# Five moves of work in a fused FFT and SoLU kernel: the last chunk's halves in one step, a fold ahead of a product, and an opening in another order

## The chip, the cores and the metric

The kernel runs on one core of a Trainium2 chip. All numbers are device microseconds (us) of that core. A core has five engines that run their own instruction queues: TensorE (PE in the profile, its weight loads PEld), VectorE (DVE), ScalarE (ACT), GpSimd (POOL) and SyncE (SP), which here only issues DMAs. An engine works through its queue in order and waits on semaphores of the others. PSUM is the memory that TensorE writes to, in banks; SBUF is the working memory.

## The reference

```python
def _attn_ref(x):                       # x: (8, 3136, 256) float32
    X = np.fft.fft(x, axis=1)
    X = np.fft.fft(X, axis=2)
    return X.real.astype(np.float32)
...
def _moe_ref(x, w_in, w_out, g_ln):     # x: (25088, 256), w_in: (256, 1024), w_out: (1024, 256)
    h = x @ w_in
    h_max = np.max(h, axis=-1, keepdims=True)
    e = np.exp(h - h_max)
    sm = e / (np.sum(e, axis=-1, keepdims=True) + 1e-09)
    solu = h * sm
    mu = np.mean(solu, axis=-1, keepdims=True)
    var = np.mean((solu - mu) ** 2, axis=-1, keepdims=True)
    ln = (solu - mu) / np.sqrt(var + 1e-06) * g_ln
    return (ln @ w_out).astype(np.float32)
```

The real part of a two-dimensional Fourier transform of eight sequences is followed by a feed-forward layer with softmax gating and a layer norm.

## The kernel before

The 3136 positions of a sequence are 49 by 64, so the long transform is done in two stages. The eight sequences are taken as four pairs (`Pair`, p = 0 to 3).

**First stage.** A pair's input comes in eight chunks of four rows (c = 0 to 7). For each chunk `load` (L117) brings the rows `xa` (a DMA of SP) and their mirror image `xb` (an indirect DMA of POOL). `add_mirror` adds the two, `fold` or `fold_part` (L164) folds the features on DVE into `y`, and `transform1` (L184) multiplies half a chunk by the table F on PE (L216) and copies the PSUM bank to `z` on ACT (L219). A pair has 16 half chunks. After a chunk's second half `keep` (L223) writes z to a DRAM tile `zd`, a DMA of SP. `turn` (L226) reads it back in another arrangement as five frequencies per tile `g`, four DMAs, usually issued by POOL (L232).

**Second stage and layer.** A pair has 25 frequencies k1, and each of these is a `Unit`, 100 in all; a unit has two signs of the frequency (one sign where k1 = 0), 128 rows each. `transform2` (L234) makes q from g on PE (L244), `take2` (L248) copies it by ACT, `spread` (L252) turns one row of q into a column r by a 0.5 KB DMA on SP. `up` (L267) multiplies q by the input weights, even part c = 0 and odd part c = 1, into two PSUM tiles h0 and h1 (L272). On DVE `even` (L275, row L278) makes ev from h0, `join` (row L286) adds and subtracts h1 and finds the extremes, ACT takes the exponential (`expo`, L294), DVE multiplies (`product`, L301), ACT squares (`square`, L308), and `stats` and `power` make the scales. DVE turns blocks of 32 by 32 (`turn_both`, L372) into a tile v, and `move_blocks` (L396) sets 16 DMAs on SP (L408) that bring the blocks of two units to their places in uT. Two tiles of tag v and two of tag uT exist.

**The way down.** From the sixth step on a unit with two signs is multiplied by the output weights in seven block products instead of eight (`Down`, p1 to p7, L446); `sums` (L433, row L439) makes their operands on POOL, `keep_p`, `keep_x`, `keep_c` and `finish` scale the results into ot, and `store` writes them out: 1 SP DMA or, for two units together, 4, and for the other sign an indirect DMA of POOL (L531).

**Order.** `tc.manual_schedule()` keeps the written order on every engine. An opening prepares the weights (`Weights`: `exponent_*`, `confine` on ACT, `narrow_*` on DVE, products of the weights in `product_in`) while pair 0 goes through the first stage. Its z goes through places that are free then: chunks 2 and 3 stand in the tile `z_u` of tag u, which `expo` uses later, 4 and 5 in the weight sums `Ws`, 6 in a tile of S, 7 in a tile of g. Then one loop step per unit: steps 0 to 4 (`WHOLE` = 4) in a simple form, where `begin(i + 1)` starts the next unit, and from step 5 a pipelined form, in which step i does the up product of unit i, transforms unit i + 2, and does the way down of unit i - 5 between them; moves of blocks stand in even steps. The last step of the simple form, step 4, ends with a `fold_part` of pair 1's first chunk, behind the transposes.

**Other pairs.** The next pair's first stage is laid into the steps by a table:

```python
    SUMS = [None] + [[f + 2 * c for c in range(NC)] for f in (3, 27, 53)]
    ...
    def ahead_pe(pr, i):
        for c in range(NC):
            half = i - SUMS[pr.p][c] - 3
            if half in (0, 1):
                transform1(pr, c * CH // 2 + half)
    ...
        at = (-4, -3, 1, 6, 11)      # turn_parts: steps of `turn`, counted from the pair's first unit
```

For pair 1 the halves of the last chunk stand in steps 20 and 21, the first `turn` in step 21, and `transform2` of its first unit, 25, in step 23. For pair 3 these are steps 70, 71, 71 and 73, and for pair 2 they are 44, 45, 46 and 48.

Of the kernel before, what the change touches and what calls it, by code (L numbers as in the profile page):

```python
# [9 lines left out]
FP32 = mybir.dt.float32  # L10
# [7 lines left out]
P = 128  # L18
# [6 lines left out]
ZR = 4 * NK  # L25
CH = 4
NC = NH // CH
# [16 lines left out]
def kernel(  # L44
# [19 lines left out]
    nc = tc.nc  # L64
# [40 lines left out]
    def result(i):  # L105

        return banks[i % 4]
# [76 lines left out]
    def transform1(pr, s):  # L184

        c, l = divmod(2 * s, CH)
        if s == 0:
            pr.zd = dram.tile([ZR, NH, D], FP32, tag="zd", name="zd")  # L190
        if l == 0:

            if pr.p or c < 2:
                pr.z = zpool.tile([ZR, CH, D], FP32, tag="z", name="z")
            elif c < 4:
                if c == 2:
                    pr.z_u = fpool.tile([P, 2, FF], FP32, tag="u", name="z_u", bufs=1)
                pr.z = pr.z_u[0:ZR, c - 2].rearrange("p (l d) -> p l d", l=CH)
            elif c < 6:
                pr.z = Ws.rearrange("p (h w) c k -> h p (w c k)", h=2)[c - 4, 0:ZR].rearrange("p (l d) -> p l d", l=CH)  # L200
            elif c == 6:
                pr.z = S_tiles[1][0:ZR, 0:2].rearrange("p a c k -> p (a c k)").rearrange("p (l d) -> p l d", l=CH)
            else:
                pr.z = gpool.tile([P, KG, D], FP32, tag="g", name="z_g")[0:ZR, 0:CH, :]
            pr.zs[c] = pr.z
        y = pr.y[c]
        ps = result(0 if pr.p else s).rearrange("p (l d) -> p l d", l=2)
        if s == NH // 2 - 1:
            parts = [(ps[0:ZR, 0], y[:, l], 0), (ps[0:ZR, 1], pr.y0[:, 0], 1), (ps[0:ZR, 1], y[:, l + 1], 2)]
        else:  # L210
            parts = [(ps[0:ZR], y[:, l : l + 2], 0)]
        pr.done.append(s)
        first = True
        for o, i, t in parts:
            for h, cs in enumerate((EVEN, ODD)):
                nc.tensor.matmul(o[..., cs], F[:, 2 * t + h, :], i[..., cs], start=first, stop=True,  # L216
                                 skip_group_check=True)
                first = False
        nc.scalar.copy(pr.z[:, l : l + 2, :], ps[0:ZR])  # L219
        if l == CH - 2:  # L220
            keep(pr, c, slice(0, ZR if pr.p else 4 * KG))
# [30 lines left out]
    def spread(t):  # L252

        t.r = small.tile([P, 1], FP32, tag="r", name="r")
        nc.sync.dma_start(out=t.r, in_=t.q[0:1, P : 2 * P])
# [3 lines left out]
    class Unit:  # L259


        def __init__(self, p, k1):
            self.p, self.k1 = p, k1
            self.signs = (0, 1) if k1 else (0,)
            self.h, self.u, self.ot = [None] * 2, [None] * 2, [None] * 2

    def up(t, c):  # L267

# [6 lines left out]
    def even(t, ps):  # L275

        t.ev = fpool.tile([P, FF], FP32, tag="ev", name="ev", bufs=1)
        nc.vector.scalar_tensor_tensor(out=t.ev, in0=w_mid, scalar=t.r, in1=ps,  # L278
                                       op0=ALU.mult, op1=ALU.add)
# [298 lines left out]
    def confine(unit, here=False):  # L578

        if unit is None:  # L580
            return
        if here:
            bits(unit, unit, -896.0, ALU.add, 0.0, ALU.max)
            bits(unit, unit, 255.0, ALU.min, 2.0 ** 23, ALU.mult)
            return

        u = unit.bitcast(FP32)
        nc.scalar.activation(out=u, in_=unit, func=ACT.Relu, bias=limits[:, 0:1])
        nc.scalar.activation(out=u, in_=u, func=ACT.Relu, bias=limits[:, 1:2], scale=-1.0)  # L589
        nc.scalar.activation(out=unit, in_=u, func=ACT.Identity, bias=limits[:, 2:3], scale=-(2.0 ** 23))  # L590
# [22 lines left out]
    class Weights:  # L613
# [40 lines left out]
        def product_in(self, h):  # L654
            ps = ps_h.tile([P, FF], FP32, tag=f"h{h % 2}", name="wps")
            for half in range(2):
                fs = slice(half * HW, (half + 1) * HW)
                for c in range(KD):
                    lhsT = self.m[:, c, :] if h == KD else self.Q[:, c, h * P : (h + 1) * P]
                    nc.tensor.matmul(ps[:, fs], lhsT, self.w_in[c][:, fs], start=(c == 0), stop=(c == KD - 1))  # L660
            nc.scalar.copy(w_mid if h == KD else Wi[:, h, :], ps)

        def place_out(self):
# [50 lines left out]
                          mybir.DependencyInfo(mybir.DependencyClass.Sync, mybir.DependencyReason.DATA),  # L714
                          reason="two operands at a time from SBUF")

    def ahead_pe(pr, i):

        for c in range(NC):
            half = i - SUMS[pr.p][c] - 3  # L720
            if half in (0, 1):
                transform1(pr, c * CH // 2 + half)

# [6 lines left out]
    with tc.manual_schedule():  # L730
# [30 lines left out]
        for c in range(NC):  # L761

            if c == 0:
                weights.narrow_in(0)
                weights.narrow_in(1)
            elif c < 3:
                weights.narrow_in(c + 1)
            if c < 2:
                weights.exponent_in(c + 2)
            add_mirror(first, c, nc.vector)  # L770
            fold(first, c)
            if c == NC - 1:
                for i in range(3):
                    weights.exponent_out(i)
            if c + 6 < NC:
                load(first, c + 6)
            if c == 3:
                weights.place_out()
                for i in range(2):
                    weights.load_out(i)  # L780
                weights.load_table(0)
                weights.mid()
                weights.scale_out()
            for s in range(CH // 2):
                transform1(first, c * CH // 2 + s)
            if c == 3:
                weights.product_in(0)

        turn(first, 0, nc.sync, 0, 2)
        turn(first, 0, nc.gpsimd, 2, KG)  # L790

        confine(weights.units[0], True)
        for i in range(1, 3):
            confine(weights.units[i])
        weights.product_in(1)
        weights.narrow_out(0)
        weights.exponent_out(3)
        weights.product_in(2)
        for i in range(1, 3):
            weights.narrow_out(i)  # L800

        units = [Unit(p, k1) for p in range(NP) for k1 in range(NK)]
        for t in units[:2]:
            take2(t, transform2(pairs[0], t.k1))
            spread(t)
        confine(weights.units[-1])
        for c in (2, 3, 0, 1, 4, 5, 6, 7):
            keep(first, c, slice(4 * KG, ZR))
        weights.load_table(1)
# [3 lines left out]
        def second_transform(i):  # L813
            if i < len(units):
                t = units[i]
                take2(t, transform2(pairs[t.p], t.k1))
                spread(t)

        def enter(i):
            cur = units[i]  # L820
# [4 lines left out]
        def begin(i):  # L825

            cur = units[i]
            enter(i)
            even(cur, up(cur, 0))
            cur.odd = up(cur, 1)  # L830
            second_transform(i + 2)

# [7 lines left out]
        for i in range(whole + 1):  # L840
            cur = units[i]
            prv = units[i - 1] if i else None
            if prv:
                turn_whole(prv)
            for s in cur.signs:
                join(cur, s)
            if prv and i < whole:
                for o, ps in prv.wait:
                    nc.vector.tensor_copy(out=o, in_=ps)
            for s in cur.signs:  # L850
                expo(cur, s)
            if prv and i == whole:
                for o, ps in prv.wait:
                    nc.scalar.copy(o, ps)
            if i == 0:

                weights.narrow_out(3)
            for s in cur.signs:
                product(cur, s)
                if i < whole and s == 0:  # L860
                    square(cur, s)
            if i == 1:
                weights.centre()
                weight_sums()
            if i < whole:

                begin(i + 1)
                if 1 in cur.signs:
                    square(cur, 1)
                stats(cur)  # L870
                power(cur)
            else:
                for s in cur.signs:
                    square(cur, s)
                other_pairs(i, ahead, "mirror", cur)
                turn_both(cur)
                stats(cur)
                power(cur)
            if i == 0:
                turn(first, 1, nc.sync)  # L880
            for work in ("mirror", "fold", "load") if i < whole else ("fold", "load"):
                other_pairs(i, ahead, work)

        def by_seven(i):
# [6 lines left out]
        for i in range(whole + 1, len(units) + lag + 1):  # L891
# [31 lines left out]
            if seven:  # L923
                new.p6()
                new.keep_x()
                new.p2()
                new.keep_c()
            elif old:
                for s, ps in plain:
                    scale(old, s, ps)  # L930
            if prv and prv.batch.shared and prv.w:
                prv.batch.mix()
            if cur:
# [119 lines left out]
```

## Time and profile before

| | us |
|---|---|
| three runs | 1149.07, 1149.42, 1147.12 (median 1149.07) |
| the profiled execution | 1150.92 |
| its span, first to last instruction | 1149.1 |
| PE busy | 1098.1 |
| DVE busy | 993.0 |
| ACT busy | 799.3 |
| POOL busy | 799.9 |

Busy time is what an engine's instructions took; the span is what all engines share, so 51 us of it are without a matmul. The mean granted TensorE clock of the execution is 0.994 of full speed. A step is measured from one unit's first up matmul (L272) to the next one's. Between disturbances it lasts 10.13 us, 11.00 us with a half chunk of the first stage in it, and 11.45 us with the last half chunk, which has six matmul operations in place of two.

### The profile page before, as it was taken

The numbers are of one execution on the slowest core, as the hardware profiler recorded it, in microseconds if no ns is written. First come the engines' busy times: TensorE is split into PE (matmuls) and PEld (weight loads), VectorE is DVE, ScalarE is ACT, GpSimd is POOL, SyncE is SP. The second block draws the span as 40 slices with busy tenths as digits, with TensorE's granted clock in tenths as the row PEclk, the third lists the DMA queues.
The fourth block names the chain that finished last, engine by engine and source line by source line (L and its number), as shares of the span: only waits on it lengthen the run. The fifth ranks groups of instructions, "written<-read, shape, count | busy, mean of one in ns | idle before, by whom it ended". The sixth has DMA issues, their size and how long they took to land.

```text
span 1149.1 us, 21936 instructions
## 1 busy us (share of the span) xinstructions
PE 1098.1 (96%) x7026; PEld 877.3 (76%) x7026; DVE 993.0 (86%) x1440; ACT 799.3 (70%) x1945; POOL 799.9 (70%) x698
## 2 busy tenths in 40 slices
PE   2988999999899999999999999999989999999998
PEld 1555787887688778778888787877868778888887
DVE  7889898898789988988888998898878999898983
ACT  4567777777566777777766777777766777777761
POOL 3036788875786888876778788876498576766673
PEclk9999999999999999999999999999999999999999
DMA  9772698776878779966869798876587676865664
GB/s 237 208 193 56 147 193 199 179 150 145 157 162 170 196 171 182 192 152 147 168 142 196 162 193 186 198 178 149 128 149 152 141 158 133 148 142 113 141 138 116
DMA packets 459889, 185.78 MB, mean 162 GB/s; under 512 B 427158, under 2 KB 441758, under 8 KB 459776
## 3 DMA queue, kind: packets, MB, share of 16 engines
q1 hardware_dynamic: 446016, 146.23, 62.1%
q0 software_dynamic: 13760, 38.16, 12.6%
q8 instruction: 57, 0.93, 0.3%
q14 instruction: 56, 0.46, 0.1%
HBM read 44.78 MB, written 38.80 MB: 73 GB/s over the span
## 4 chain that ended last, share of the span: by engine, by line
PE 85%; DMA 5%; DVE 4%; issue 2%; ACT 2%; POOL 1%; SPq 1%; POOLq 0%; DVEq 0%
PE ps_m L446 49%; PE ps_h L272 27%; PE ps_m L216 4%; PE ps_m L244 4%; DMA room<-in_x_dram 2%; DMA g<-zd 1%; DVE h L286 1%; DVE u L301 1%; DMA F<-in_f_tab_dram 1%; ACT h L308 1%; PE wps L660 1%; POOL S L439 0%; DVE ev L278 0%; DVE y L150 0%; DMA zd<-z 0%
## 5 line engine op out<-in xcount | busy, mean ns | idle before, releaser
L272 PE MATMUL ps_h<-Wi,q 128*128 128x512 f32 x800 | 363.3, 596 | 7.7 <-DVE nmax L286 4.5
L439 POOL TENSOR_TENSOR S<-uT 128x512 f32<-128x512 f32 x186 | 240.0, 1290 | 97.4 <-DVE u L301 38.8
L446 PE MATMUL ps_m<-Ws,S 128*128 128x128 f32 x2304 | 297.0, 275 | 0.6 <-POOL xa L142 0.6
L446 PEld LDWEIGHTS ps_m<-Ws,S 128*128 128x128 f32 x2304 | 280.6, 192 | 3.9 <-POOL xa L142 0.7
L308 ACT ACTIVATE h<-u,usum 128x1024 f32<-128x1024 f32 x196 | 225.0, 1149 | 83.6 <-DVE u L301 81.3
L272 PEld LDWEIGHTS ps_h<-Wi,q 128*128 128x128 f32 x800 | 144.7, 191 | 155.4 <-issue 141.5
L301 DVE SCALAR_TENSOR_TENSOR u<-h,u 128x1024 f32<-128x1024 f32 x196 | 239.1, 1256 | 7.2 <-ACT u L294 7.1
L294 ACT ACTIVATE u<-h,nmax 128x1024 f32<-128x1024 f32 x196 | 223.3, 1141 | 8.8 <-DVE nmax L286 5.8
L372 DVE STREAM_TRANSPOSE v<-u 128x2048 f32<-128x2048 f32 x88 | 203.4, 2311 | 3.0
L446 PE MATMUL ps_m<-Wo,uT 128*128 128x128 f32 x1536 | 205.0, 277 | 0.4 <-DMA out_dram<-ot 0.4
L446 PEld LDWEIGHTS ps_m<-Wo,uT 128*128 128x128 f32 x1536 | 188.9, 193 | 1.5 <-issue 1.5
L286 DVE CUSTOM_DVE_ANT_0 h<-ev,ps_h 128x1024 f32<-128x1024 f32 x100 | 122.1, 1221 | 17.3 <-DVE ev L278 8.6
L531 POOL DMA_INDIRECT out_dram<-ot,idx x96 | 109.5, 1141 | 36.5 <-issue 11.3
L286 DVE CUSTOM_DVE_ANT_0 h<-h,ps_h 128x1024 f32<-128x1024 f32 x96 | 117.3, 1221 | 13.8
L278 DVE SCALAR_TENSOR_TENSOR ev<-w_mid,r,ps_h 128x1024 f32<-128x1024 f32 x100 | 124.1, 1241 | 2.9 <-ACT S L589 2.4
L439 POOL TENSOR_TENSOR S<-S,uT 128x512 f32<-128x512 f32 x93 | 120.6, 1297 | 7.3
L439 POOL TENSOR_TENSOR S<-uT,S 128x512 f32<-128x512 f32 x93 | 119.7, 1287 | 7.3
L244 PEld LDWEIGHTS ps_m<-T,g 128*128 128x128 f32 x400 | 60.0, 191 | 60.1 <-issue 55.9
L446 PE MATMUL ps_m<-Ws,uT 128*128 128x128 f32 x768 | 103.6, 279 | 0.0
L446 PE MATMUL ps_m<-Wo,S 128*128 128x128 f32 x768 | 101.5, 275 | 0.8 <-ACT ot L481 0.8
L216 PE MATMUL ps_m<-y,F 98*100 98x258 f32 (+3 forms) x288 | 72.8, 389 | 23.9 <-DVE y L162 23.9
L446 PEld LDWEIGHTS ps_m<-Ws,uT 128*128 128x128 f32 x768 | 95.6, 195 | 0.0
(101 smaller groups left out, 1174.3 us busy)
## 6 DMA issues: line engine op xcount, KB each, us to landing
uT<-v SPq DMA_DIRECT2D x752, 128.0 KB
g<-zd POOLq DMA_DIRECT2D x72, 160.0 KB, 4.6
out_dram<-ot SPq DMA_DIRECT2D x176, 64.0 KB
xa<-in_x_dram SPq DMA_DIRECT2D x28, 392.0 KB
zd<-z SPq DMA_DIRECT2D x24, 400.0 KB
raw_in<-in_moe_w_in_dram SPq DMA_DIRECT2D x4, 512.0 KB
raw_out<-in_moe_w_out_dram SPq DMA_DIRECT2D x2, 1024.0 KB
r<-q SPq DMA_DIRECT2D x100, 0.5 KB
```

Of the source, the lines that this page charges most:

```text
L216: nc.tensor.matmul(o[..., cs], F[:, 2 * t + h, :], i[..., cs], start=first, stop=True, skip_group_check=True)
L244: nc.tensor.matmul(o, g[:, k, h * P : (h + 1) * P], table, start=(h == 0), stop=True, skip_group_check=True)
L272: nc.tensor.matmul(ps[:, fs], t.q[:, c * P : (c + 1) * P], Wi[:, c, fs], start=True, stop=True)
L278: nc.vector.scalar_tensor_tensor(out=t.ev, in0=w_mid, scalar=t.r, in1=ps, op0=ALU.mult, op1=ALU.add)
L286: nc.vector.tensor_tensor_reduce(out=t.h[s], in0=t.h[0] if s else t.ev, in1=t.odd, scale=1.0 if s else -0.5, scalar=3.0e38, op0=ALU.add, o ...
L294: nc.scalar.activation(out=t.u[s], in_=t.h[s], func=ACT.Exp, bias=t.nmax[:, s : s + 1], scale=-1.0, accum_out=t.esum[:, s : s + 1])
L301: t.last = nc.vector.scalar_tensor_tensor(out=t.u[s], in0=t.h[s], scalar=-1.0, in1=t.u[s], op0=ALU.mult, op1=ALU.mult, accum_out=t.usum[:, ...
L308: nc.scalar.activation(out=t.h[s], in_=t.u[s], func=ACT.Square, bias=t.usum[:, s : s + 1], scale=-float(FF), accum_out=t.ssq[:, s : s + 1])
L372: nc.vector.transpose(out=t.batch.v[:, :, t.w], in_=t.both.rearrange("p s (g n) -> p (s g) n", n=32))
L439: i = engine.tensor_tensor(out=S[j], in0=a, in1=b, op=op)
L446: nc.tensor.matmul(o, a[:, c], b[:, c], start=start and c == 0, stop=c == n - 1, skip_group_check=True)
L531: dma = nc.gpsimd.indirect_dma_start(out=out, out_offset=bass.IndirectOffsetOnAxis(ap=idx[:, i : i + 1], axis=0), in_=t.ot[s], in_offset=None)
```

## The change

Pair 0's z of chunks 2 to 5 goes into one tile `z_v` of tag v. For each later pair both halves of the last chunk stand in one step: the first half where it stood, the second further back in the same step (`late`), behind p2. In step 4 the fold is done ahead of the product. In the opening the three products of the weights change order, the fourth piece of the output weights is narrowed there and no longer in step 0, and `begin(1)` comes ahead of the first `product`. For units 2 and 3 `spread` is replaced by `column`: a matmul with a single one turns the row of q into a PSUM column, and DVE copies it.

```diff
-            elif c < 4:
+            elif c < 6:
                 if c == 2:
-                    pr.z_u = fpool.tile([P, 2, FF], FP32, tag="u", name="z_u", bufs=1)
-                pr.z = pr.z_u[0:ZR, c - 2].rearrange("p (l d) -> p l d", l=CH)
-            elif c < 6:
-                pr.z = Ws.rearrange("p (h w) c k -> h p (w c k)", h=2)[c - 4, 0:ZR].rearrange("p (l d) -> p l d", l=CH)
+                    pr.z_v = fpool.tile([P, 2, FF, 2], FP32, tag="v", name="z_v", bufs=2)
+                pr.z = pr.z_v[0:ZR].rearrange("p a f b -> p (a f b)").rearrange("p (c l d) -> p c l d", c=4, l=CH)[:, c - 2]
...
+    def column(t):
+
+        ps = result(2)[:, 0:1]
+        nc.tensor.matmul(ps, t.q[0:1, P : 2 * P], ones[0:1, 0:1], start=True, stop=True)
+        t.r = small.tile([P, 1], FP32, tag="r", name="r")
+        nc.vector.tensor_copy(out=t.r, in_=ps)
...
+            return ps
+
+        def keep_in(self, h, ps):
             nc.scalar.copy(w_mid if h == KD else Wi[:, h, :], ps)
...
-    def ahead_pe(pr, i):
+    def ahead_pe(pr, i, late=False):
 
         for c in range(NC):
             half = i - SUMS[pr.p][c] - 3
+            if c == NC - 1:
+                half = int(late) if half == 0 else None
+            elif late:
+                half = None
             if half in (0, 1):
                 transform1(pr, c * CH // 2 + half)
...
+        middle = weights.product_in(KD)
         confine(weights.units[0], True)
         for i in range(1, 3):
             confine(weights.units[i])
-        weights.product_in(1)
+        weights.keep_in(KD, middle)
         weights.narrow_out(0)
         weights.exponent_out(3)
-        weights.product_in(2)
-        for i in range(1, 3):
+        confine(weights.units[-1])
+        odd = weights.product_in(1)
+        for i in range(1, 4):
             weights.narrow_out(i)
 
         units = [Unit(p, k1) for p in range(NP) for k1 in range(NK)]
         for t in units[:2]:
             take2(t, transform2(pairs[0], t.k1))
             spread(t)
-        confine(weights.units[-1])
+            if t is units[0]:
+                weights.keep_in(1, odd)
...
-                spread(t)
+                if i not in (2, 3):
+                    spread(t)
...
-            even(cur, up(cur, 0))
+            ps = up(cur, 0)
+            if i in (2, 3):
+                column(cur)
+            even(cur, ps)
...
             if i == 0:
-
-                weights.narrow_out(3)
+                begin(1)
+            if i == whole:
+                other_pairs(i, ahead, "fold")
             for s in cur.signs:
                 product(cur, s)
...
-                begin(i + 1)
+                if i:
+                    begin(i + 1)
...
-            for work in ("mirror", "fold", "load") if i < whole else ("fold", "load"):
+            for work in ("mirror", "fold", "load") if i < whole else ("load",):
                 other_pairs(i, ahead, work)
...
+            if cur:
+                other_pairs(i, ahead_pe, True)
             if prv and prv.batch.shared and prv.w:
                 prv.batch.mix()
```

## The prediction

> **What bounds the kernel now.** First the page: which engine is full, and what the chain of work that ended last is made of.
>
> ```profile
> PE 1098.1 (96%) x7026; PEld 877.3 (76%) x7026; DVE 993.0 (86%) x1440; ACT 799.3 (70%) x1945; POOL 799.9 (70%) x698
> PE 85%; DMA 5%; DVE 4%; issue 2%; ACT 2%; POOL 1%; SPq 1%; POOLq 0%; DVEq 0%
> ```
>
> TensorE is the bound, so a change pays only where PE waits or runs slowly. I then measured every step (first L272 to first L272). From step 7 on they are 10.13, 11.00 or 11.45 us, within 0.15 us, apart from those around the units of one sign and two single ones, step 23 (294.11 to 310.91, 16.81 us) and step 73 (833.74 to 849.80, 16.06 us). The table of stretches shows what is in them.
>
> ```profile
> core 0: us, PE busy (x) PEld busy (x) DVE busy (x) ACT busy (x) POOL busy (x), PEclk, DMA share, GB/s
> 105.10:118.30 13.20, 13.19 (x75) 10.01 (x76) 11.77 (x18) 8.96 (x24) 11.87 (x13) 0.87 0.45 123
> 283.97:294.11 10.14, 10.14 (x71) 8.23 (x70) 9.05 (x12) 6.97 (x20) 1.06 (x2) 1.00 0.47 112
> 294.11:310.90 16.79, 11.98 (x70) 9.75 (x69) 11.73 (x12) 8.29 (x19) 16.23 (x16) 0.90 1.13 190
> 833.74:849.80 16.06, 12.00 (x71) 9.77 (x69) 10.21 (x12) 8.31 (x19) 15.50 (x17) 0.89 1.19 192
> ```
>
> Steps 23 and 73 hold the same 70 or so matmuls as step 22, but PE is empty for 4.8 and 4.1 us and the granted clock falls to 0.90 and 0.89: an idle stretch is paid twice. The timeline gives the cause at the first of them.
>
> ```profile
> 270.97 13.52 SPq L408 DMA_DIRECT2D uT<-v  x16
> 280.60 0.59 ACT L219 COPY z<-ps_m 100x512 f32<-100x512 f32 x1 [0.79 <-PE ps_m L216]
> 281.46 0.99 POOL L531 DMA_INDIRECT out_dram<-ot,idx  x1 [0.15 <-issue]
> 284.60 3.06 SPq L539 DMA_DIRECT2D out_dram<-ot  x4
> 288.41 0.47 SPq L224 DMA_DIRECT2D zd<-z  x1
> 293.05 2.40 POOL L232 DMA_DIRECT2D g<-zd  x4 [10.60 <-DMA zd<-z]
> 302.51 0.68 PE L244 MATMUL ps_m<-T,g 128*128 128x128 f32 x4 [4.81 <-DMA g<-zd]
> ```
>
> z is complete at 281.19, but the `keep` of it stands in SP's queue behind 16 moves and 4 stores and goes out at 288.41; POOL, whose next instruction is the `turn`, waits 10.60 us for it to land; g is late for unit 25 by 4.81 us. Step 73 repeats it.
>
> Last the end of step 4 and step 5, on DVE and PE:
>
> ```profile
> 98.23 2.31 DVE L372 STREAM_TRANSPOSE v<-u 128x2048 f32<-128x2048 f32 x1
> 100.46 0.60 DVE L149 TENSOR_TENSOR y<-xa 98x254 f32<-98x254 f32 x1
> 100.73 1.70 POOL L439 TENSOR_TENSOR S<-uT 128x512 f32<-128x512 f32 x1
> 100.98 1.72 DVE L150 TENSOR_TENSOR y<-xa 98x254 f32<-98x254 f32 x1
> 102.63 1.23 DVE L174 TENSOR_TENSOR y<-xa,xb 98x2 f32<-98x2 f32 x1
> 103.78 1.27 DVE L278 SCALAR_TENSOR_TENSOR ev<-w_mid,r,ps_h 128x1024 f32<-128x1024 f32 x1
> 105.11 5.38 PE L272 MATMUL ps_h<-Wi,q 128*128 128x512 f32 x8 [2.95 <-DVE ev L278]
> ```
>
> PE needs h0 back from `even` of unit 5, which stands behind the fold; the fold takes 3.3 us beside POOL's sums (0.98 us for the same three rows at 107.74, where POOL only issues DMAs). PE idles 2.95 us, and the eight up matmuls then take 5.38 us in place of 3.60.
>
> **The change part by part.**
>
> *Last chunk in one step (pairs 1, 2, 3).* The built order shows six matmul operations, one copy of z and one `keep` moved from steps 21, 45, 71 to 20, 44, 70; on SP the `keep` now stands ahead of the 16 moves, and POOL's order is the same. Work is equal: step 20 becomes 11.00 + (11.45 - 10.13) = 12.32 us, step 21 10.13. With S the start of step 20, p2 ends at S + 9.4 (270.90 - 261.52), the second half runs to S + 10.8, z is copied by S + 11.4 and the `keep` issued by S + 11.9. Before, issue to POOL's release took 4.64 us, so zd is there at S + 16.5. POOL reaches the `turn` 9.9 us after step 21's start (282.45 - 272.52), at S + 22.3: it no longer waits. Its DMAs are issued by S + 24.8. Landing took 7.1 us at most, so g is there by S + 31.9. PE asks for it 3.44 us into step 23, at S + 36.0. Margin 4 us: both stalls go whole, (16.81 - 10.13) + (16.06 - 10.13) = 12.6 us.
> What is now queued behind the waiting `keep`: the 16 moves start 2.5 us later. They took 13.5 us, so they land near S + 28, and the sums of step 22 on POOL, due at S + 25.6, start 2.4 us late and end by S + 33.5, before the next product on DVE (S + 34) and before p5 of step 23 (S + 38). Nothing on the path; cover about 4 us, beyond it 1:1. In step 20 `expo` stands behind the second copy of z and starts 1.7 us later, 0.4 us later than the longer step; `even` comes 5.7 us into a step and PE feels it only past about 7.9 (10.13 + 1.72 for h0's matmuls - 3.94 for even and join). Zero. For pair 2 the `turn` comes a step after the `keep` and nothing waits; late sums cost POOL's `turn` there some 0.9 us of a 2 us margin: zero, at worst 0.5.
>
> *Step 4's fold.* The join ends at 95.36, POOL's mirror at 95.63, the exponential at 95.7. Fold 95.65 to 96.5, products to 98.8, transpose to 101.1, `even` to 102.4. PE has finished its other work at 102.15, so it restarts at 102.4 and not 105.11: 2.7 us. Next the clock. The Trainium skill ("TensorE: Matmul & The Clock Gate", Part 1, What's actually happening) says that the clock halves after an idle window of about 3.4 us that runs freely; by that rule a 2.95 us gap might not have cooled PE and only 2.7 us return. The row says it did: 0.87 over 13.20 us is 1.7 us lost, and steps 5 to 6 are too long by as much. I take the row; the gap left is 0.3 us. Together 4.4 us.
> Against it speaks "GPSIMD Engine Reference" (Specifications, SBUF interfaces): GpSimd shares its interface to SBUF with VectorE instructions of two SBUF inputs. The fold is such a one, and step 5's fold now comes at 105.05 with the sums of step 5 running from 101.3 to 106.5, where it had been clear of them. If it is held as in the rows above (3.3 us), `join` of unit 6 ends at about 117.2, h1 comes back 1.7 us late, and 2.7 us are left. Only the last of the four sums overlaps, so I take 1 us of delay: join ends at 115.7, PE asks for h1 at 115.5. 0.1 us lost; 4.3 us stay, 2.7 as the lower end.
>
> *Opening.* In step 0 `narrow_out(3)` (62.82 to 65.47, 2.65 us on DVE) goes to the gap ahead of `even` of unit 0. That gap is
>
> ```profile
> 60.02 1.28 DVE L278 SCALAR_TENSOR_TENSOR ev<-w_mid,r,ps_h 128x1024 f32<-128x1024 f32 x1 [2.35 <-ACT S L589]
> ```
>
> 2.35 us, so it fills it and `even` starts at 60.3. ACT has `confine` (2.2 us) ahead of q instead of behind: q at 57.6 and not 57.4, so the up products of both units are 0.2 us later. `product` of unit 0 now follows `even` of unit 1, which waits for its up matmul until 64.0: it starts at 65.3 against 65.47. So DVE's 2.65 us are mostly spent in a new wait, and the chain goes on through ACT (square, stats, copies, exponential). There q of unit 3 (0.35 us) is now copied ahead of the square, in an idle place: 0.45 us. The tile of tag u no longer waits for the `keep`, but the product was held by DVE to 65.4 anyway: zero, as for `Ws`, whose first write at 76.12 waits for DVE.
> `column` replaces two 0.5 KB DMAs by a matmul of one column and a DVE copy of 128 x 1. No row is that small; 0.15 us, as for the 98 x 2 rows of L174, twice. It takes away the 0.39 us that `even` of unit 2 waited at 76.04. Opening in all: 0.4 us gained, between a loss of 0.8 (ACT's new order late by 1 us) and a gain of 1.2.
>
> *Sum.* 12.6 + 4.3 + 0.4 = 17.3 us off the profiled 1150.92 (span 1149.1 and 1.8 around it) is 1133.6. The median of the runs is 1149.07, 0.16% below the profiled one: 1131.8.
>
> **The rivals.**
>
> *A part of the stalls stays.* The `turn` lands later than before because moves, stores and it now share the DMA engines in other order. For it: the DMA share of 1.13 and 1.19 in the two stretches above. Against: the 4 us margin. With 2 us of PE idle left at each place and no slow clock, 4 us are lost: 1136. With the clock, 1139.
>
> *VectorE takes over behind step 4.* The held fold above, and opening gain zero: 1.6 + 0.4 us lost, 1134.
>
> *Slower: the balance of the steady steps tips.* All 93 later steps hold because DVE's products fall between POOL's sums. Where they overlapped once, at 295.09, product took 2.75 and 2.28 us in place of 1.22. The changed start brings DVE into step 6 at 9.3 us after PE's up matmul, where it was 8.0. If that lag stayed and each step lost more than 17.3 / 93 = 0.19 us, the kernel is slower; at 0.3 us each it is 1131.8 + 28 = 1160. Against it: before, a lag of 8.0 in step 6 was 6.0 one step later, and step 24 is 10.13 straight after the stall. DVE has 9.05 us of work in a step of 10.14.
>
> *It does not do what it says.* The `keep` could still be behind other DMAs; the built order excludes that.
>
> **How the numbers follow.** All three gains nearly whole, 1131.8: 0.70. VectorE behind step 4, 1134: 0.12. Stalls in part, 1136 to 1139: 0.13. Slower, 1160: 0.03. The same, where several losses meet: 0.02. The range runs from 1129.5 (opening at its best, and the 1 us by which the three runs scatter) to 1137.5, which leaves out the worst of the partial stalls and the slow case. About 0.2%, 2.3 us, is what a measurement of this kernel can tell from no change. Faster 0.95, same 0.02, slower 0.03.
>
> **What would show it.** Right: steps 23 and 73 at 10.13 with clock 1.00, step 20 at 12.32, no wait of POOL for zd, PE restarting near 102 with clock 1.00 up to the next step. Wrong: an L244 that still waits for g, POOL's sums on top of DVE's products in steps 22 or 72, a wait of PE on `join` in steps 6 to 8, or steady steps above 11.00.

## The result, and the profile after

| | median, us | lowest to highest | runs |
|---|---|---|---|
| kernel before | 1149.24 | 1147.12 to 1149.64 | 4 |
| changed kernel | 1134.99 | 1132.91 to 1139.53 | 4 |

The ratio is 0.9885, 95% interval 0.9852 to 0.9918: between 9.4 and 17.0 us faster, 14.25 by the medians. The forecast was 1131.8 in a range of 1129.5 to 1137.5, so the median lies 3.2 us above it and inside the range. The profiled execution took 1132.91 us with a span of 1130.9 and a mean granted clock of 1.00; before it was 0.994.

In the changed kernel the lines have other numbers: `up` is L277, `even` L283, `join` L291, `product` L306, `transform1` L214 and L217, `keep` L222, `turn` L230, `transform2` L242, moves L413, `sums` L444, the stores of SP L544 and L546, `column` L268 and L270. First the page's row of busy times and its row of the chain by engine:

```profile
PE 1092.3 (97%) x7030; PEld 872.2 (77%) x7030; DVE 987.4 (87%) x1442; ACT 800.5 (71%) x1945; POOL 796.3 (70%) x698
PE 90%; DVE 4%; issue 2%; ACT 2%; DMA 2%; SPq 0%; POOL 0%; POOLq 0%; DVEq 0%; ACTq 0%
```

PE is busy 5.8 us less with the same work (and two matmuls of one column), as less of it runs at a low clock: by the rows of the prediction the low clock cost 0.13 x 13.20 + 0.10 x 16.79 + 0.11 x 16.06 = 5.2 us in steps 6, 23 and 73. DMA's share of the chain falls from 5% to 2%: the waits for g are gone. The table of stretches, for steps 5, 6, 23 and 73 (columns as in the prediction's table):

```profile
90.39:100.09 9.70, 8.11 (x28) 4.85 (x28) 9.05 (x13) 8.69 (x23) 5.40 (x5) 1.00 0.01 0
100.09:113.29 13.20, 11.95 (x75) 9.35 (x75) 12.58 (x16) 9.17 (x26) 12.57 (x13) 1.00 0.53 123
289.14:299.27 10.13, 10.13 (x70) 8.22 (x69) 9.12 (x12) 8.12 (x19) 9.57 (x11) 1.00 0.93 180
821.89:832.02 10.13, 10.13 (x70) 8.22 (x69) 9.09 (x12) 8.12 (x19) 9.74 (x11) 1.00 0.93 188
```

Steps 23 and 73 are now steps like all others, with PE full. Step 6 is the line to stop at: its clock is 1.00 and no longer 0.87, yet it takes 13.20 us as before.

Where the 18.2 us between the two spans went, by the start of each step:

| stretch | before | after | gain |
|---|---|---|---|
| start to step 5 | 92.64 | 90.39 | 2.25 |
| step 5 | 12.46 | 9.70 | 2.76 |
| step 6 | 13.15 | 13.20 | -0.05 |
| steps 20 and 21 | 11.00 + 11.45 | 12.32 + 10.13 | 0 |
| step 23 | 16.81 | 10.13 | 6.68 |
| step 73 | 16.06 | 10.13 | 5.93 |

That is 17.6. Another 0.3 us are in the last stretch, from the last of the up products to the end (45.2 against 44.9 us), and 0.6 in step 29 (11.10 against 10.54 us), whose length scatters from profile to profile (see "The sum"). The other steps together lose 0.3.

The timeline of steps 20 to 23 shows the new order at the first of the two stalls (start, duration, engine and line, what, and in brackets the idle time before it):

```profile
267.28 0.59 ACT L217 COPY z<-ps_m 100x512 f32<-100x512 f32 x1 [0.95 <-PE ps_m L214]
267.90 0.29 SPq L222 DMA_DIRECT2D zd<-z  x1
268.35 14.84 SPq L413 DMA_DIRECT2D uT<-v  x16
279.02 2.42 POOL L230 DMA_DIRECT2D g<-zd  x4
282.74 1.27 POOL L444 TENSOR_TENSOR S<-uT 128x512 f32<-128x512 f32 x1 [1.30 <-PE ps_h L277]
292.57 0.61 PE L242 MATMUL ps_m<-T,g 128*128 128x128 f32 x4
```

The `keep` follows the copy of z by 0.03 us. The `turn` has no bracket any more: POOL does not wait for zd. The matmul on g has none either.

The timeline of steps 5 and 6 shows why step 6 gave nothing back:

```profile
93.42 0.42 DVE L149 TENSOR_TENSOR y<-xa 98x254 f32<-98x254 f32 x1 [0.31 <-POOL xa L142]
98.80 1.24 DVE L283 SCALAR_TENSOR_TENSOR ev<-w_mid,r,ps_h 128x1024 f32<-128x1024 f32 x1
100.09 1.98 PE L277 MATMUL ps_h<-Wi,q 128*128 128x512 f32 x4 [0.18 <-DVE ev L283]
102.73 0.86 DVE L149 TENSOR_TENSOR y<-xa 98x254 f32<-98x254 f32 x1
102.96 1.96 PE L277 MATMUL ps_h<-Wi,q 128*128 128x512 f32 x4 [0.88 <-DVE nmax L291]
103.28 1.22 POOL L444 TENSOR_TENSOR S<-uT 128x512 f32<-128x512 f32 x1
103.52 1.25 DVE L150 TENSOR_TENSOR y<-xa 98x254 f32<-98x254 f32 x1
108.72 1.11 PE L214 MATMUL ps_m<-y,F 98*100 98x258 f32 x4 [0.36 <-ACT q L248]
```

The fold of step 4 is clear of POOL now (0.42 us for its first row), and PE idles 0.18 us for `even` in place of 2.95. But then the second up product waits 0.88 us for `join` of unit 5, and the first-stage matmul waits 0.36 us for a copy of q. The two together are the idle time of the step: 13.20 - 11.95 = 1.25 us. The next fold, at 102.73, runs beside the sums and takes 0.86 and 1.25 us for two rows that took 0.42 us each in the fold of step 4.

### The profile page after: what moved, and what is told of

Its sections match the earlier page's. It is cut to its first block, busy times and chain, and to the rows that moved or that the text cites. A ratio compares the mean times of both kernels' runs of the same rounds, so it can differ in the third digit from the quotient of the medians.

```text
span 1130.9 us, 21944 instructions
## 1 busy us (share of the span) xinstructions
PE 1092.3 (97%) x7030; PEld 872.2 (77%) x7030; DVE 987.4 (87%) x1442; ACT 800.5 (71%) x1945; POOL 796.3 (70%) x698
## 3 DMA queue, kind: packets, MB, share of 16 engines
q0 software_dynamic: 13760, 38.16, 13.1%
## 4 chain that ended last, share of the span: by engine, by line
PE 90%; DVE 4%; issue 2%; ACT 2%; DMA 2%; SPq 0%; POOL 0%; POOLq 0%; DVEq 0%; ACTq 0%
PE ps_m L451 52%; PE ps_h L277 28%; PE ps_m L214 5%; PE ps_m L242 4%; DMA raw_in<-in_moe_w_in_dram 1%; DVE h L291 1%; DVE u L306 1%; PE ps_m L519 1%; ACT h L313 1%; DVE ev L283 0%; DVE y L150 0%; PE wps L665 0%; DVE Wo L615 0%; DVE y L149 0%; ACT u L299 0%
## 5 line engine op out<-in xcount | busy, mean ns | idle before, releaser
L277 PE MATMUL ps_h<-Wi,q 128*128 128x512 f32 x800 | 362.4, 594 | 5.9 <-DVE nmax L291 5.1
L444 POOL TENSOR_TENSOR S<-uT 128x512 f32<-128x512 f32 x186 | 238.0, 1279 | 108.3 <-DVE u L306 34.5
L277 PEld LDWEIGHTS ps_h<-Wi,q 128*128 128x128 f32 x800 | 143.8, 190 | 152.0 <-issue 139.4
L306 DVE SCALAR_TENSOR_TENSOR u<-h,u 128x1024 f32<-128x1024 f32 x196 | 234.7, 1234 | 9.4 <-ACT u L299 9.4
L291 DVE CUSTOM_DVE_ANT_0 h<-ev,ps_h 128x1024 f32<-128x1024 f32 x100 | 122.2, 1222 | 17.0 <-DVE ev L283 8.8
L536 POOL DMA_INDIRECT out_dram<-ot,idx x96 | 109.7, 1143 | 37.4 <-issue 12.5
L291 DVE CUSTOM_DVE_ANT_0 h<-h,ps_h 128x1024 f32<-128x1024 f32 x96 | 117.2, 1221 | 14.2 <-DVE nmax L291 0.5
L283 DVE SCALAR_TENSOR_TENSOR ev<-w_mid,r,ps_h 128x1024 f32<-128x1024 f32 x100 | 124.1, 1241 | 0.8 <-PE ps_h L277 0.7
L444 POOL TENSOR_TENSOR S<-uT,S 128x512 f32<-128x512 f32 x93 | 118.8, 1278 | 7.3
L444 POOL TENSOR_TENSOR S<-S,uT 128x512 f32<-128x512 f32 x93 | 118.7, 1277 | 7.3
L242 PEld LDWEIGHTS ps_m<-T,g 128*128 128x128 f32 x400 | 60.1, 191 | 50.1 <-issue 45.7
L451 PEld LDWEIGHTS ps_m<-Wo,S 128*128 128x128 f32 x768 | 93.4, 192 | 1.0 <-issue 1.0
L214 PE MATMUL ps_m<-y,F 98*100 98x258 f32 (+3 forms) x288 | 70.4, 377 | 24.4 <-DVE y L162 22.1
```

The costliest lines, as they stand in the source:

```text
L242: nc.tensor.matmul(o, g[:, k, h * P : (h + 1) * P], table, start=(h == 0), stop=True, skip_group_check=True)
L277: nc.tensor.matmul(ps[:, fs], t.q[:, c * P : (c + 1) * P], Wi[:, c, fs], start=True, stop=True)
L291: nc.vector.tensor_tensor_reduce(out=t.h[s], in0=t.h[0] if s else t.ev, in1=t.odd, scale=1.0 if s else -0.5, scalar=3.0e38, op0=ALU.add, o ...
L306: t.last = nc.vector.scalar_tensor_tensor(out=t.u[s], in0=t.h[s], scalar=-1.0, in1=t.u[s], op0=ALU.mult, op1=ALU.mult, accum_out=t.usum[:, ...
L444: i = engine.tensor_tensor(out=S[j], in0=a, in1=b, op=op)
L451: nc.tensor.matmul(o, a[:, c], b[:, c], start=start and c == 0, stop=c == n - 1, skip_group_check=True)
```

## The experiments

Two groups ran, each beside its own runs of the kernel before: medians 1149.45 (23 runs) for the first four, 1150.67 (23 runs) for the last four. Medians and the ratios of the comparison differ by up to 2 us as gains, so both are given.

**e1_late: the kernel before with only the last chunk's halves in one step.**

```diff
-    def ahead_pe(pr, i):
+    def ahead_pe(pr, i, late=False):
...
             half = i - SUMS[pr.p][c] - 3
+            if c == NC - 1:
+                half = int(late) if half == 0 else None
+            elif late:
+                half = None
...
+            if cur:
+                other_pairs(i, ahead_pe, True)
             if prv and prv.batch.shared and prv.w:
```

> The kernel before with only the last chunk's two halves in one step. As predicted: steps 23 and 73 fall from 16.81 and 16.06 to 10.13 us, 12.6 us gained, about 1136.6 where before is 1149.2. Rival (the stalls go only together with the other edits, or part stays because transfers land later): less than 9 us, and an L244 that still waits for g.

Measured: 1139.87 (6 runs), ratio 0.9899 (0.9875 to 0.9922), which is 9.0 to 14.4 us; 9.6 by the medians. Steps 20 to 24 are 12.32, 10.13, 10.13, 10.13, 10.13 us, and steps 70 to 74 the same. Both stalls go whole with this edit alone, and it is most of the change. The gain by the medians is 3.0 us short of the 12.6 that were expected.

**e2_fold: the kernel before with only step 4's fold moved.**

```diff
+            if i == whole:
+                other_pairs(i, ahead, "fold")
             for s in cur.signs:
                 product(cur, s)
...
-            for work in ("mirror", "fold", "load") if i < whole else ("fold", "load"):
+            for work in ("mirror", "fold", "load") if i < whole else ("load",):
```

> The kernel before with only step 4's fold moved ahead of the product. By the prediction's sum 4.3 us (2.7 for the earlier restart, 1.7 for the clock). Theory from the trace after: 2.7 us only, because the clock of step 6 is full again but the second up matmul of step 6 then waits for join of unit 5 (0.9 us) and a first-stage matmul for ACT (0.4 us); steps 5 and 6 about 9.7 and 13.2 us, granted clock 1.00 in step 6.

Measured: 1147.56 (12 runs), ratio 0.9977 (0.9958 to 0.9996): 0.5 to 4.8 us, 1.9 by the medians. Steps 5 and 6 take 9.69 and 13.19 us. So the earlier restart is there (12.46 - 9.69 = 2.8), and the clock's part is not: step 6 keeps its length in this kernel too, without any of the other edits.

**e3_open: the kernel before with only the opening.**

```diff
-            elif c < 4:
+            elif c < 6:
...
+                    pr.z_v = fpool.tile([P, 2, FF, 2], FP32, tag="v", name="z_v", bufs=2)
...
-                spread(t)
+                if i not in (2, 3):
+                    spread(t)
...
+                begin(1)
...
```

> The kernel before with only the opening's edits (z of chunks 2 to 5 in a tile of tag v, order of the weight products, begin(1) ahead of the first product, r of units 2 and 3 by TensorE). By the prediction 0.4 us gained. If the 2.25 us by which the opening was shorter in the profile after is its work: 2.3 us. If that is only the arrival of the first inputs: 0 to 0.5 us from the fold of chunk 4 to step 5, whatever the arrival.

Measured: 1148.47 (12 runs), ratio 0.9980 (0.9958 to 1.0001), 1.0 us by the medians. The runs alone hardly tell this from nothing. The timeline, with a shorter stretch to measure, does better; it is read below.

**e4_all: the changed kernel again, beside its parts.**

> The changed kernel once more, beside its parts on the same chip. Sum of the parts if they add: 12.6 + 2.7 + 0.4 = 15.7 us by the trace, 17.3 by the prediction; the time at which chunk 4's inputs arrive on DVE (36.49 before, 34.24 after) should differ from run to run without the code having a part in it.

Measured: 1136.87 (6 runs), ratio 0.9874 (0.9851 to 0.9897), 12.6 us by the medians. The three parts sum to 9.6 + 1.9 + 1.0 = 12.5 by the medians (11.6 + 2.6 + 2.3 = 16.5 by the ratios, against 14.5). Within these intervals no loss or gain between the parts can be told.

**e5_keep_old_place: the changed kernel, with the `keep` of the last chunk at its old place in SP's queue.** Both halves stay in one step. It tells the place of the `keep` from the place of the matmuls.

```diff
-            keep(pr, c, slice(0, ZR if pr.p else 4 * KG))
+            if not pr.p or c < NC - 1:
+                keep(pr, c, slice(0, ZR if pr.p else 4 * KG))
...
                 other_pairs(i, ahead_pe)
+                if cur.p + 1 < NP and i == SUMS[cur.p + 1][NC - 1] + 4:
+                    keep(pairs[cur.p + 1], NC - 1, slice(0, ZR))
```

> The changed kernel, but the keep of the last chunk goes back to its old place on SP (steps 21, 45, 71, behind 16 moves and 4 stores), while both halves stay in steps 20, 44, 70. If the place in SP's queue is the cause of the stalls: they come back, steps 23 and 73 at 13 to 17 us as in the kernels without the edit, some 10 us slower than the changed kernel, and POOL waits about 10 us for zd. If it is the second half's computation that was late: no wait, the time of the changed kernel (1135 to 1137).

Measured: 1147.87 (12 runs), ratio 0.9978 (0.9960 to 0.9996). The stalls are back: step 23 takes 16.91 us, step 73 16.46. Its timeline:

```profile
268.65 0.58 ACT L217 COPY z<-ps_m 100x512 f32<-100x512 f32 x1 [0.95 <-PE ps_m L214]
284.77 0.52 SPq L223 DMA_DIRECT2D zd<-z  x1
289.45 2.41 POOL L231 DMA_DIRECT2D g<-zd  x4 [9.07 <-DMA zd<-z]
298.19 1.19 PE L243 MATMUL ps_m<-T,g 128*128 128x128 f32 x4 [4.08 <-DMA g<-zd]
```

z is complete at 269.23, and its write goes out 15.5 us later. Everything after that is the old picture: POOL waits 9.07 us, PE 4.08. What made the stalls was the place of one DMA in SP's queue; making z earlier without it brings nothing at these places. By the ratios, each to its own runs of the kernel before (0.9978 here, 0.9885 and 0.9874 for the changed kernel), that place is worth 10.7 to 12.0 us.

**e6_filler: the kernel before, with six matmuls of unused results in step 5.** They keep PE busy in the gap ahead of step 6, so that the clock is not lowered while the gap in the chain stays.

```diff
+                for k in range(6 if i == whole + 1 else 0):
+                    nc.tensor.matmul(result(2)[:, 0:D], ident, Wo[:, k, :], start=True, stop=True, skip_group_check=True)
```

> The kernel before with six extra matmuls (128x256, about 2.7 us, results not used) in step 5 behind the way down of unit 0, where PE idled 2.95 us. This keeps the clock up and moves nothing else. By the prediction's step the slow clock costs 1.7 us there, so step 6 falls from 13.15 to about 11.4. By the theory that a wait on join of unit 5 stands right behind it: the granted clock of step 6 is 1.00, but the second up matmul of step 6 waits for DVE, and step 6 falls only to 12.3 to 12.7.

Measured: 1148.69 (12 runs), ratio 0.9986 (0.9971 to 1.0002). The table of stretches has step 6 of it (columns as above):

```profile
104.23:116.80 12.57, 11.69 (x74) 9.27 (x75) 11.71 (x18) 8.89 (x24) 11.81 (x13) 1.00 0.46 130
```

and its timeline the two places where PE waits around it:

```profile
104.23 1.99 PE L272 MATMUL ps_h<-Wi,q 128*128 128x512 f32 x4 [0.36 <-DVE ev L278]
107.10 1.96 PE L272 MATMUL ps_h<-Wi,q 128*128 128x512 f32 x4 [0.88 <-DVE nmax L286]
```

The clock is 1.00, and only 0.6 us of step 6 come back in place of the 1.7 that the clock had cost. With a quick PE, `join` (it makes nmax) is late by 0.88 us. At the low clock PE came late itself, and the wait could not be seen. The wait of 0.36 us for q is not in this kernel: its step-5 fold is clear of the sums.

**e7_fold5: the changed kernel, with step 5's fold behind the transposes**, so that it no longer meets the sums.

```diff
-                other_pairs(i, ahead, "fold")
+                if i > whole + 1:
+                    other_pairs(i, ahead, "fold")
...
                 turn_both(cur)
+                if i == whole + 1:
+                    other_pairs(i, ahead, "fold")
```

> The changed kernel with step 5's fold moved behind the transposes, clear of POOL's sums. By the theory that its collision with the sums (2.3 us in place of 1.0) delays product and, through ACT's square, the copy of q of unit 8, for which a first-stage matmul waits 0.4 us: that wait goes and step 6 falls from 13.2 to about 12.8; the 0.9 us wait on join stays. Rival: even of unit 6 comes later by the fold (1 us) and PE waits in step 7 instead: no gain.

Measured: 1139.72 (6 runs), ratio 0.9909 (0.9884 to 0.9934). Its stretches of steps 6 and 7:

```profile
102.23:114.82 12.59, 11.71 (x74) 9.29 (x75) 11.97 (x16) 9.30 (x26) 10.39 (x11) 1.00 0.37 99
114.82:129.80 14.98, 12.97 (x75) 10.63 (x73) 13.52 (x18) 8.60 (x21) 14.16 (x11) 0.89 1.07 171
```

Step 6 falls to 12.59 us, as the filler says it must. Step 7 goes up to 14.98, from 11.14 in the changed kernel. Two rows of the timeline say how:

```profile
106.47 2.05 DVE L306 SCALAR_TENSOR_TENSOR u<-h,u 128x1024 f32<-128x1024 f32 x1
123.65 1.29 PE L214 MATMUL ps_m<-y,F 98*100 98x258 f32 x4 [2.00 <-ACT q L248]
```

With the fold out of the way, `product` itself meets the sums (2.05 us in place of 1.22). The sums end later, the next sums with them, and these meet the next fold; at the end of that chain PE waits 2.00 us for a copy of q, and the clock goes to 0.89. The collision was not taken away but handed on, at 3.8 us for 0.6; about 1.6 of the 3.8 are the low clock (0.11 x 14.98). The rival named beforehand expected a wait in step 7 too, but for `even`.

**e8_both: e7, and in step 6 the transform of unit 8 between the two up products**, to cover the wait for `join`.

```diff
                 even(cur, up(cur, 0))
+                if i == whole + 2:
+                    second_transform(i + 2)
                 cur.odd = up(cur, 1)
-                second_transform(i + 2)
+                if i != whole + 2:
+                    second_transform(i + 2)
```

> As the run with step 5's fold behind the transposes, and in step 6 the transform of unit 8 stands between the two up matmuls, in the place where PE waits 0.9 us for join. If the wait on join is what is left of the 1.7 us: step 6 falls by another 0.6 us to about 12.2, 1.0 us below the changed kernel's 13.2; in the median at the edge of what can be told. Rival: the later work is bound by DVE anyway and steps 6 and 7 together stay as they were.

Measured: 1138.34 (6 runs), ratio 0.9901 (0.9878 to 0.9924). Steps 6 and 7 take 12.55 and 15.05 us. The 0.6 us expected of step 6 did not come: the wait for `join` falls from 0.88 to 0.44 us, but a first-stage matmul later in the step now waits 0.16 us for a copy of q, and the step is 0.04 us shorter than in e7. By the ratios neither e7 nor e8 is better than the changed kernel (0.9885 and 0.9874).

## Why the prediction was right, and where not

**The stalls: mechanism right, size from one profile.** Each step of the working was found close to where it was put, counted from the start of step 20 at 256.55: z copied at 11.3 (forecast 11.4), `keep` issued at 11.4 (11.9), the `turn` reached at 22.5 (22.3), g asked for at 36.0 (36.0) and there in time. The late moves cost nothing: the sums of step 22 begin at 26.2, earlier than the 28 allowed for, and end at 31.4, ahead of the next product. Steps 20 and 23 are 12.32 and 10.13, to the hundredth. e5 shows the cause directly.
The term of 12.6 us stood for the one profile of before exactly, and for the runs it was probably too large. Five profiles of kernels with the `keep` in its old place (before, e2, e3, e5, e6) have stalls of 12.6, 8.3, 10.0, 13.1 and 11.0 us over two plain steps. Their mean is 11.0, and it belongs against the medians. I had corrected for the distance of that profile from the median, 0.16%, as if this removed its chance part; it did not. The 9.0 to 14.4 us of e1 hold both 11.0 and 12.6.

**Step 4's fold: the clock's term failed.** The restart came as worked out: 100.09 is 102.4 less the 2.25 us by which this profile started earlier. That term, 2.7, was measured as 2.8. The 1.7 us of clock were the error. I read 0.87 over 13.20 us as time that would come back with the clock. The clock did come back, in the changed kernel, in e2 and in e6, and step 6 stayed at 13.2 or fell by 0.6 at most. Without the low clock and with step 5's fold clear of the sums, as in e6 and e7, step 6 takes 12.57 and 12.59 us, with 0.88 us of idle PE ahead of the second up product. How much of the 1.7 us that wait for `join` takes can be read from the start of the step to its `transform2`: 5.22 us at the low clock (before), 4.66 with the wait at the full clock (e6, e7 and the changed kernel), 3.44 with neither (step 22 of the changed kernel). The low clock costs 1.8 us there, but 1.2 of them lie over a wait that a slow PE hid, and only 0.6 can come back. This 0.6 is lost again in the changed kernel, where step 5's fold meets the sums. I had seen this collision and had followed it only to the `join` of unit 6; by the timeline it goes through `product`, `square` and the copy of q to the first-stage matmul of the same step. The lower end of 2.7 is what was measured, but I had reached it by another path, a `join` of unit 6 that comes late; that it agrees is luck. A wait of PE on `join` in steps 6 to 8 was on my list of what would show me wrong.

**The opening: right in sign, and in size as far as can be told.** I took 0.4 us. From the narrowing on DVE just ahead of the first mirror-add in the tile `room` to step 5, the four profiles with the old opening take 65.4 us in the mean (64.5 to 67.0), the six with the new one 64.5 (64.1 to 64.9): 1.0 us, and 0.6 in the profiled pair. But the 67.0 us are e1's, where PE waited 1.92 us for a DMA in step 3 and the clock then fell (0.87 over the step); without this profile the old opening takes 64.9 us, and the gain is 0.5. Three rows of the changed kernel's timeline:

```profile
58.98 1.27 DVE L283 SCALAR_TENSOR_TENSOR ev<-w_mid,r,ps_h 128x1024 f32<-128x1024 f32 x1
62.33 1.28 DVE L283 SCALAR_TENSOR_TENSOR ev<-w_mid,r,ps_h 128x1024 f32<-128x1024 f32 x1 [0.70 <-PE ps_h L277]
73.95 1.28 DVE L283 SCALAR_TENSOR_TENSOR ev<-w_mid,r,ps_h 128x1024 f32<-128x1024 f32 x1
```

This profile runs 1.63 us ahead of the one of before at that narrowing (25.71 and 27.34), so 1.63 is added to compare. `even` of unit 0 comes at 60.6 (forecast 60.3): the narrowing of the fourth piece fills the gap of 2.35 us and a little more. `even` of unit 1 waits for its up product, as expected, until 63.96 (64.0). `column`'s copy takes 0.15 us, the price taken over from the 98 x 2 rows, and `even` of unit 2 follows at once; it is 14.97 us behind that of unit 0, where before it was 16.41. The forecast's parts were there. The runs themselves, -0.1 to 4.8 us by e3's interval, can't tell 0.4 from 1.0.

**The sum.** For the runs, 11.0 + 2.8 and 0.5 to 1.0 for the opening make 14.3 to 14.8 us, against 14.25 and 12.6 in the two measurements by medians, 13.2 and 14.5 by ratios. I had 17.3; 1.6 of the excess are the stalls' and 1.5 the clock's. The medians lie inside the forecast because its range reached 5.7 us above its centre; that of the repeat, e4, at 1136.87, is 0.6 us from that end. The profiled pair came near my sum, 18.2 us, with the help of chance: 1.6 us of it are the 1.63 us above, by which it was ahead in code that the change does not touch, and 0.6 are step 29.
I had left step 29 out. PE waits there, by up to 2.2 us, for POOL, whose sums had waited 2.75 us (changed kernel) to 4.75 us (e1) for a DMA. Five profiles with the `keep` in its new place have 10.54 to 14.32 us for this step (12.1 in the mean), five with the old place 11.10 to 12.09 (11.3). Whether the change has a part in this 0.8 us, or chance alone, stays open.

**The rivals.** That a part of the stalls stays is out: no profile with the `keep` in the new place has them. VectorE behind step 4 did take over, as the `join` that PE had been too slow to notice and as the held fold; this rival's total, 1134, is as near to the median of 1134.99 as the 1136 of the partial stalls, which did not happen: the totals alone don't tell my cases apart, the steps do. The slower case did not come: from step 7 on the steps are as before, apart from those named (183.80 us for steps 7 to 28 without 20 to 24, in both kernels). e7 shows its beginning, 3.8 us in one step, and that the steps after it recover.

## What to carry to other kernels

A transfer's place in the in-order queue that issues it can cost more than its transfer: ask what stands ahead of it there, and move that place before moving the work. Time at a low clock is not time that comes back with the clock; find first the wait that the slow engine hides. And where an accident repeats in a trace, measure its size in several profiles before it goes into a sum against a median.

## What was not expected of the hardware

The length of a gap did not decide whether PE's clock went down. Gaps of PE of 2.95 us (before, step 6), 3.01 (e2, step 23) and 2.00 (e7, step 7) were followed by 0.87 to 0.89 over their step, gaps of 2.59 (e3, step 73) and 3.15 (e2, step 73) by 1.00. The same 70 or so matmuls take 11.99 us in step 23 of e2 and 10.37 in step 73.

What decides it can be read from the clock that the ten traces record. Whenever it falls while the kernel works, it falls to one half, for 3.41 us or twice that, and every fall lies a whole number of times 3.413 us after the moment from which that profile first shows the full clock. Cut into windows at these times, e2 shows both cases (columns as in the tables above):

```profile
296.09:299.50 3.41, 1.29 (x11) 1.32 (x12) 3.38 (x3) 1.94 (x5) 3.33 (x3) 1.00 1.32 163
299.50:302.91 3.41, 3.41 (x18) 3.41 (x17) 3.09 (x5) 0.94 (x4) 3.19 (x5) 0.50 1.40 169
831.97:835.38 3.41, 1.51 (x4) 0.38 (x2) 3.41 (x3) 1.24 (x2) 3.25 (x3) 1.00 1.14 217
835.38:838.79 3.41, 2.16 (x19) 2.19 (x20) 3.38 (x4) 2.13 (x6) 3.41 (x3) 1.00 1.41 167
```

Most of the gap of 3.01 us lies in one window, which has 1.29 us of busy PE, and the next one runs at half the clock. The gap of 3.15 us is cut in two by a window's edge, 1.51 and 2.16 us of busy PE are left, and the clock stays. Over the ten profiles, of the 3219 windows at the full clock, each of the 24 with up to 1.41 us of busy PE was followed by half the clock, and none with 1.50 us or more; of the two between, one was. This fits the freely running window that the Trainium skill describes ("TensorE: Matmul & The Clock Gate", Part 1, What's actually happening), in which it matters how a gap lies to the window; its length of about 3.4 us is no safe bound here. The page speaks of an idle window, but here a window with 1.41 us of work in it was enough. The windows lie otherwise in each execution, so for a forecast a gap of 2 to 3.2 us is a chance of some 1.7 us (half of 3.41), and this is a part of the scatter of the stalls.

The first inputs arrive at times of their own. In ten profiles the narrowing named above starts between 25.7 and 29.3 us, ahead of anything that the edits touch; why was not settled. A difference of under 2 us between two single profiles of this kernel may be just that.
